# Engines lay out q and k, and the seven-product experts get other rooms, routes and an order

## Chip, core, metric

One core of a Trainium2 chip. The metric is device time in microseconds (us) of one execution of the whole program. TensorE (PE) does matmuls and transposes, VectorE is DVE, ScalarE is ACT, GpSimd is POOL, and SyncE (SP) issues every DMA of this program, in order.

## What is computed

The program is top-32 attention, a SiLU feed-forward layer, and eight ReLU experts weighted by a Sinkhorn-balanced gate, in fp32 precision.

```python
# q, k, v: (2, 8, 576, 64)
scores = q @ k.T / 8                       # per batch and head, 576 x 576
kth    = 32nd largest of each row
attn   = softmax(where(scores >= kth, scores, -1e9))
x      = (attn @ v) laid out as (1152, 512)
h = x @ w_in;  x = (h * sigmoid(h)) @ w_out          # 512 -> 2048 -> 512, float64 weights in DRAM
P = exp(x @ w_gate - max)                             # (1152, 8)
8 times: P /= row sums; P /= column sums; P *= 1152/8
out = sum over e of P[:, e] * (relu(x @ w1[e]) @ w2[e])   # 512 -> 1024 -> 512
```

## The kernel before, in words

**Attention** runs in 24 units (`units`, L589) of up to four score tiles; a unit is one pair of heads of one batch and one slice of query rows. For each score tile DVE finds the top 32 by four MAX8 and three MATCH_REPLACE (L304, L310), masks (L313), and ACT and PE do the rest. `load` brings q, k and v of a unit two units ahead. `turn_kv` and `turn_q` put q and k into the form that `score_tile` wants one unit ahead: two heads side by side, the fp32 value split into a high part (H, written by ACT) and the rest (L, written by DVE). PE transposes the natural tile, ACT and DVE empty PSUM into `kH, kL, qH, qL`, and then DMAs on the SP queue copy these from SBUF to SBUF into `kk`, `qq` and `qLz` (L236, L277 to L283). Only the first pair, named in `DIRECT`, is written by the engines directly.

**Feed-forward and experts of the early tokens.** There are nine token tiles of 128 rows. m0 (`row_ffn`, L640) is the layer for tile 0; it reads float64 weights, narrows them (`narrow`) and stores them in DRAM as `kept_in`, `kept_out`. Then `FILL[g]` follows after each group: six experts for tile 0 by `row_ffn`, then m1 (tiles 1, 2), expert 6 for tile 0 and expert 0 for tiles 1, 2, then m2 (tiles 3, 4) and expert 0 for tiles 3, 4. All of these use the same three PSUM `banks`, so on PE they follow each other in this order; this is called the chain of layers here. m3 (tiles 5 to 8) follows when attention is over. Then come the gate's Sinkhorn iterations (L720), and `AFTER`: expert 7 for tile 0 and expert 0 for tiles 5 to 8. Outputs of experts that can't be weighted yet go to DRAM (`ky`, L672, L778).

**The seven-product experts** (`ORDER`, L907): experts 7 to 1 on tiles 1 to 8, with the first layer done in blocks by seven products in place of eight. `pair_weights` loads raw weights (`raw_tile`, tag `raw`), forms sums on POOL (L810 to L813) and splits them into `wp` and `w2`. `pair_hidden` runs the seven products in the four PSUM banks `hb`; `first_half` and the loop over `yB` run the second layer. In the second of these experts (`i == 1`) all kept outputs are read back (`yk`, L913) through a pool of two tiles (`x1p`) and added on DVE (`weighted`, L892).

**What sets the order.** Tile writes each engine's instruction stream when the program is built, from priorities (`tc.cur_priority`, lower is earlier) and a modelled time; on the chip each stream runs in order. Work at `uid() * 100` comes first, then attention at 10 to 34 GAP, the layers, `AFTER` at 112 GAP, and `ORDER` at 300 GAP. Products of one expert have one priority, so the streams mix them.

Of the kernel before, what the change touches and what calls it, by code (L numbers as in the profile page):

```python
# [8 lines left out]
F32 = mybir.dt.float32  # L9
# [8 lines left out]
P = 128  # L18
# [6 lines left out]
    0: [(e, [0], "rows") for e in range(6)],  # L25
    1: [(6, [0], "rows"), (0, [1, 2], "split")],
# [7 lines left out]
DIRECT = [(0, 0)]  # L34

# [3 lines left out]
RW = 6  # L39
RWL = 5  # L40
# [4 lines left out]
KB = 2  # L45
# [17 lines left out]
def topk_attention_moe_sinkhorn_kernel(  # L63
# [121 lines left out]
    qq_half = [qtp.tile([P, 2, P], F32R, name=f"qq_half{i}", tag=f"qq_half{i}", bufs=1) for i in range(2)]  # L185
    qL_half = [qtp.tile([P, 2, P], F32R, name=f"qL_half{i}", tag=f"qL_half{i}", bufs=1) for i in range(2)]

    qLz = [qtp.tile([P, 2, 2 * P], F32R, name=f"qLz{i}", tag=f"qLz{i}", bufs=1) for i in range(2)]
    for t in qq_half + qL_half + qLz:
        nc.gpsimd.memset(t.bitcast(F32), 0.0)  # L190
    half_no = [0]
    full_no = [0]
# [16 lines left out]
    def turn_kv(b, p, kn, vn):  # L209

        kk = kvp.tile([P, 2, S], F32R, name=f"kk_{b}_{p}", tag="kk")
        direct = (b, p) in DIRECT
# [10 lines left out]
        if not direct:  # L223
            kH = nat.tile([P, S], F32R, name=f"kH_{b}_{p}", tag="kH", bufs=KB)
            kL = nat.tile([P, S], F32R, name=f"kL_{b}_{p}", tag="kL", bufs=KB)
# [7 lines left out]
        for src, hh in () if direct else ((kH, 0), (kL, 1)):  # L233
            for j in range(2):
                o = (j + hh) % 2 * 64
                nc.sync.dma_start(kk.bitcast(F32)[o : o + 64, j, :], src.bitcast(F32)[j * 64 : (j + 1) * 64, :])  # L236
        return kk, vn

    def load_q(b, p, t0, n, half):
        qn = nat.tile([P, 2, 2, D], F32, name=f"qn_{b}_{p}_{t0}", tag="qn")  # L240
        for j in range(2 if n else 0):
            nc.sync.dma_start(
                qn[:, 0:n, j, :],
                q[b, 2 * p + j, 0 : 4 * P, :].rearrange("(p c) d -> p c d", c=4)[:, t0 : t0 + n, :],
            )
        if half:
            nc.sync.dma_start(qn[0:64, 1, :, :], q[b, 2 * p : 2 * p + 2, 4 * P : S, :].rearrange("h p d -> p h d"))
        return qn

    def turn_q(b, p, t0, n, half, qn):  # L250

        w = n * P + (64 if half else 0)
        pq = ps_p.tile([P, 2 * P], F32, name=f"pq_{b}_{p}_{t0}", tag="pp")
        for c in range(n):
            nc.tensor.transpose(pq[:, c * P : (c + 1) * P], qn[:, c, :, :].rearrange("p h d -> p (h d)"), ident)
        if half:
            nc.tensor.transpose(pq[:, n * P : w], qn[0:64, 1, :, :].rearrange("p h d -> p (h d)"), ident[0:64, 0:64])
        low = qLz[full_no[0] % 2]
        full_no[0] += n > 0
        qq = qtp.tile([P, 2, 2 * P], F32R, name=f"qq_{b}_{p}_{t0}", tag="qq") if n else None  # L260
        if (b, p) in DIRECT and t0 == 0 and not half:
            for j in range(2):
                r = slice(j * 64, (j + 1) * 64)
                for o in (0, 64):
                    nc.scalar.activation(qq[o : o + 64, j, :w], pq[r, :w], AF.Copy)
                nc.vector.tensor_sub(low[r, j, :w], pq[r, :w], qq[r, j, :w].bitcast(F32))
            return qq, low, None
        qH = qtp.tile([P, 2 * P], F32R, name=f"qH_{b}_{p}_{t0}", tag="qH")
        qL = qtp.tile([P, 2 * P], F32R, name=f"qL_{b}_{p}_{t0}", tag="qL")
        evac_split(qH[:, :w], qL[:, :w], pq[:, :w])  # L270
        i = half_no[0] % 2
        half_no[0] += half
        for j in range(2):
            r = slice(j * 64, (j + 1) * 64)
            for o in (0, 64):
                if n:
                    nc.sync.dma_start(qq.bitcast(F32)[o : o + 64, j, : n * P], qH.bitcast(F32)[r, : n * P])  # L277
                if half:
                    nc.sync.dma_start(qq_half[i].bitcast(F32)[o : o + 64, j, r], qH.bitcast(F32)[r, n * P : w])
            if n:  # L280
                nc.sync.dma_start(low.bitcast(F32)[r, j, : n * P], qL.bitcast(F32)[r, : n * P])
            if half:
                nc.sync.dma_start(qL_half[i].bitcast(F32)[r, j, r], qL.bitcast(F32)[r, n * P : w])  # L283
        return qq, low, (qq_half[i], qL_half[i])
# [164 lines left out]
    def first_blocks():  # L449
# [5 lines left out]
        for i in (*range(13, nb), *reversed(range(13))):  # L455
            got[i] = cvp.tile([P, W], F32, name=f"wf_{i}", tag=f"wf{i}", bufs=1)
# [159 lines left out]
    for u, unit in enumerate(units):  # L616
# [19 lines left out]
        if g == 0:  # L636
# [49 lines left out]
    sk = left_pool("sk", bufs=2)  # L686
    m3s = ExitStack()
# [75 lines left out]

    for n, (e, ets) in enumerate(AFTER):
        tc.cur_priority = (112 + n) * GAP
        if ets == [0]:
            ys = [banks[2]]
            row_ffn(f"e{e}", x1F, ys[0], hidB(), expert_blocks(e), DFE // W, False, hp, hidB)
        else:
            ys = ys4  # L770
            ffn(f"e{e}_{ets[0]}", [x1_cols(ets)], ys, lambda f, m: fill_weights(e, f, "late"),
                DFE // P, False, hidB, hpB, late=True, depth=1)
        tc.cur_priority = uid() * 100
        for tt, y in zip(ets, ys):
            yo = x1p.tile([P, DM], F32, name=f"yo_{e}_{tt}", tag="x1")
            nc.scalar.activation(yo, y, AF.Copy)
            kept_y[e, tt] = drp.tile([P, DM], F32, name=f"ky_{e}_{tt}")
            nc.sync.dma_start(kept_y[e, tt], yo)  # L778
# [11 lines left out]
    wpp = left_pool("wpp", bufs=2)  # L790
    gbp = left_pool("gbp", bufs=NF)
    spp = left_pool("spp")
    rwl = left_pool("rwl", bufs=RWL)
# [46 lines left out]
    def pair_hidden(e, f, wd, hb, gB):  # L840

        nm = f"{e}_{f}"
        kept = tc.cur_priority

        def add(tag, a, ps, pool=upp, bufs=1):
            tc.cur_priority = uid() * 100
# [5 lines left out]
        block_product(hb[0], wd["a11"], b11)  # L852
        tc.cur_priority = uid() * 100
# [9 lines left out]
        block_product(hb[0], wd["a12"], b21, True)  # L863
        tc.cur_priority = uid() * 100
# [3 lines left out]
        h21 = add("h21", u2, hb[2])  # L868
# [11 lines left out]
    begun = set()  # L880

    def weighted(e, tt, y):

        p_ = pr[:, tt, e : e + 1]
        if tt not in begun:
            begun.add(tt)
# [19 lines left out]

    for i, e in enumerate(ORDER):  # L907
        tc.cur_priority = (300 + i) * GAP
        weights = [pair_weights(e, f) for f in range(NH)]
        if i == 1:  # L910
            for ek, tt in kept_y:
                yk = x1p.tile([P, DM], F32, name=f"yk_{ek}_{tt}", tag="x1")
                nc.sync.dma_start(yk, kept_y[ek, tt])  # L913
                weighted(ek, tt, yk)
# [4 lines left out]
        def first_half():  # L919
            f, gs, w2s = pend.pop(0)  # L920
            for n, (g, w) in enumerate(zip(gs, w2s)):
                product(yA, w, *g, f == 0 and n == 0, f == NH - 1 and n == 1)

        for f in range(NH):
            hb = group_of(i % 2, f"h_{e}_{f}")
# [46 lines left out]
```

## Time and profile before

| | us |
|---|---|
| median of 3 runs | 1327.61 (1327.47 to 1332.26) |
| profiled execution | 1326.74 |
| its span, first to last instruction | 1325.0 |
| PE busy | 1216.8 (92%) |
| DVE busy | 860.6 (65%) |
| ACT busy | 605.7 (46%) |
| POOL busy | 518.1 (39%) |
| mean busy share of the 16 DMA engines | about 39% |

The shares of the whole span hide the stages. In the slices of the page DVE is at 9 tenths up to about slice 16 while PE climbs, then PE alone is near full. PE's granted clock is at 5 tenths in the first slices and near full later. The rows below are read stage by stage.

### The profile page before, as it was taken

Reading aid. Unit: us, or ns where it says so; the run is one execution under the profiler, and the core shown is the slowest. Engines: PE = TensorE matmul, PEld = TensorE weight load, DVE = VectorE, ACT = ScalarE, POOL = GpSimd, SP = SyncE. Lnnn points to the kernel's source line nnn. Section 1 sums busy time; section 2 is a strip of 40 time slices with the busy share of each in tenths; the row PEclk is TensorE's granted clock in tenths of the full one; section 3 lists DMA queues with packets and bytes.
Section 4 is the critical chain, followed back from the end, with each engine's and each line's share of the span. In section 5 each row is a group of like instructions: output and inputs, shape, how many; then the busy total and the mean of one; then the engine's idle time right before and its main releaser. Section 6 shows DMA issues by size and latency. Waiting matters only on the chain.

```text
span 1325.0 us, 17423 instructions
## 1 busy us (share of the span) xinstructions
PE 1216.8 (92%) x5891; PEld 934.4 (71%) x5891; DVE 860.6 (65%) x1705; ACT 605.7 (46%) x1170; POOL 518.1 (39%) x464
## 2 busy tenths in 40 slices
PE   3669799979889988999998898999999999999998
PEld 2445455557758776889667686888888888888887
DVE  6999796979999999344474645445454454544533
ACT  4777454657768877543333323232232322323211
POOL 1443000016727766622353634335344353442510
PEclk7559799989999999999999999999999999999999
DMA  6999776665454533433422513112121121211101
GB/s 156 266 320 274 226 252 187 216 180 157 127 183 127 163 104 91 138 99 97 134 80 92 163 48 112 48 32 80 32 64 49 32 80 32 64 48 32 56 1 63
DMA packets 157288, 155.82 MB, mean 118 GB/s; under 512 B 34320, under 2 KB 109200, under 8 KB 157200
## 3 DMA queue, kind: packets, MB, share of 16 engines
q1 hardware_dynamic: 157200, 154.73, 39.0%
q8 instruction: 46, 0.75, 0.2%
q14 instruction: 42, 0.34, 0.1%
HBM read 128.73 MB, written 14.94 MB: 108 GB/s over the span
## 4 chain that ended last, share of the span: by engine, by line
PE 70%; DVE 12%; DMA 9%; ACT 4%; issue 2%; SPq 2%; POOL 1%; DVEq 0%; ACTq 0%; POOLq 0%
PE h L136 9%; PE h L138 8%; PE h L137 8%; PE bank L493 4%; PE yA L136 4%; PE yA L137 4%; DVE m L304 4%; PE yA L138 4%; DVE w L310 3%; PE yB L136 3%; PE yB L137 3%; PE bank L500 3%; PE yB L138 3%; PE bank L136 2%; PE bank L138 2%; PE bank L137 2%
## 5 line engine op out<-in xcount | busy, mean ns | idle before, releaser
L128 POOL TENSOR_TENSOR wp<-rw,wp 128x512 fp32r<-128x512 f32 (+1 forms) x56 | 83.4, 1508 | 183.6 <-ACT wp L127 183.6
L128 POOL TENSOR_TENSOR wa<-raw,wa 128x512 fp32r<-128x512 f32 x72 | 95.1, 1322 | 136.5 <-ACT wa L127 119.6
L304 DVE MAX8 m<-w 128x8 f32<-128x576 f32 x192 | 140.1, 746 | 0.2
L128 POOL TENSOR_TENSOR w<-rw,w 128x512 fp32r<-128x512 f32 x56 | 80.8, 1454 | 121.0 <-ACT w L127 120.5
L127 ACT ACTIVATE w<-rw 128x512 fp32r<-128x512 f32 x56 | 35.0, 629 | 133.6 <-PE yB L138 77.5
L310 DVE MATCH_REPLACE8 w<-m,w 128x576 f32<-128x576 f32 x128 | 94.6, 740 | 0.0
L447 POOL TENSOR_TENSOR wf<-wf,cv_n 128x512 int32<-128x512 int32 x32 | 43.0, 1344 | 83.2 <-ACT cv_n L444 35.1
L136 PE MATMUL h<-x1H,wp 128*128 128x512 f32 x168 | 68.1, 405 | 7.1 <-ACT p L855 6.8
L128 POOL TENSOR_TENSOR wb<-raw,wb 128x512 fp32r<-128x512 f32 x48 | 65.8, 1373 | 21.3 <-ACT wb L127 21.3
L835 DVE SCALAR_TENSOR_TENSOR gL_1b<-gB,gH_1b 128x512 fp32r<-128x512 f32 x28 | 38.4, 1371 | 50.7 <-issue 41.4
L137 PE MATMUL h<-x1L,wp 128*128 128x512 f32 x168 | 67.1, 400 | 0.0
L138 PE MATMUL h<-x1H,wp 128*128 128x512 f32 x168 | 67.1, 399 | 0.0
L313 DVE SCALAR_TENSOR_TENSOR s<-s,m,e 128x576 f32<-128x576 f32 x64 | 61.1, 955 | 0.2
L848 DVE TENSOR_TENSOR u<-p,h 128x512 f32<-128x512 f32 x28 | 19.2, 686 | 64.5 <-ACT p L855 64.5
L304 DVE MAX8 m<-s 128x8 f32<-128x576 f32 x64 | 48.0, 749 | 19.9 <-ACT s L296 19.9
L500 PE MATMUL bank<-wa,x1F 128*128 128x512 f32 x112 | 54.6, 623 | 6.3 <-DMA wa<-in_moe_w_dram 6.3
L127 ACT ACTIVATE wb<-raw 128x512 fp32r<-128x512 f32 x72 | 45.5, 632 | 30.2 <-PE y L138 15.9
L493 PE MATMUL bank<-wb,gT_e 128*128 128x512 f32 x128 | 58.2, 596 | 0.2 <-ACT gT_e L518 0.2
L330 PE MATMUL pav<-aT,vn 128*64 128x256 f32 (+3 forms) x480 | 53.0, 363 | 5.6 <-ACT aT L333 5.5
L308 ACT ACTIVATE e<-s,sm 128x576 f32<-128x576 f32 x64 | 49.7, 776 | 15.5 <-DVE s L313 12.2
L848 DVE TENSOR_TENSOR gB<-u,h 128x512 f32<-128x512 f32 x56 | 38.5, 687 | 25.3 <-PE h L138 23.4
L320 PE MATMUL pt<-ident,s 128*128 128x128 f32 x256 | 45.1, 305 | 9.2 <-ACT s L317 6.6
(355 smaller groups left out, 3757.1 us busy)
## 6 DMA issues: line engine op xcount, KB each, us to landing
rw<-in_moe_w_dram SPq DMA_DIRECT2D x112, 256.0 KB, 2.7
wa<-in_moe_w_dram SPq DMA_DIRECT2D x32, 512.0 KB, 4.7
wb<-in_moe_w_dram SPq DMA_DIRECT2D x32, 512.0 KB, 5.3
raw<-kept_in SPq DMA_DIRECT2D x48, 256.0 KB, 3.0
raw<-kept_out SPq DMA_DIRECT2D x48, 256.0 KB, 2.7
raw<-in_moe_w_dram SPq DMA_DIRECT2D x48, 256.0 KB, 2.8
wfr<-in_moe_w_in_dram SPq DMA_DIRECT2D x16, 512.0 KB, 5.0
wfr<-in_moe_w_out_dram SPq DMA_DIRECT2D x16, 512.0 KB, 6.1
```

The lines of the kernel that those rows point to most:

```text
L127: nc.scalar.activation(dH, src, AF.Copy)
L128: eng.tensor_sub(dL, src, dH.bitcast(F32))
L136: nc.tensor.matmul(ps, wH, xH, start=first, stop=False, skip_group_check=more)
L137: nc.tensor.matmul(ps, wH, xL, start=False, stop=False, skip_group_check=more)
L138: nc.tensor.matmul(ps, wL, xH, start=False, stop=last, skip_group_check=more)
L304: nc.vector.max(mr, src)
L310: nc.vector.match_replace(out=w, in_to_replace=mr, in_values=src, imm_value=-3e38)
L313: nc.vector.scalar_tensor_tensor(s, s, m8[:, TOPK - 1 : TOPK], e, op0=ALU.is_ge, op1=ALU.mult, accum_out=sm[:, 1:2])
L330: nc.tensor.matmul(ps[r, :n], vn[:, j, c, :], aT[j][:, c, :n], start=c == 0, stop=c == 4)
L493: nc.tensor.matmul(y, gT[:, c * P : (c + 1) * P], b[c], start=F == 0 and c == 0, stop=F == nF - 1 and c == NDC - 1)
L500: nc.tensor.matmul(ph, xF[:, c, :], a[c], start=c == 0, stop=c == NDC - 1)
L848: nc.vector.tensor_add(t, a, ps)
```

## The change

It has two parts that share no code.

In attention, `turn_kv` writes every pair of `k` straight from PSUM into `kk` as `DIRECT` did for one: each column range takes two ACT and two DVE instructions on 64 partitions in place of one each on 128, and the four DMA copies go. `turn_q` first lets POOL write each head's natural rows twice side by side (`qd`), so that a PE transpose brings the head out on both halves of the partitions; PE does a transpose per head and 128 rows in place of one for both heads, ACT and DVE empty twice the columns straight into `qq` and `qL`, and all DMA copies go. The natural q rows of a unit come by one DMA in place of two.

In the layers, expert 6 for tile 0 moves from behind m1 to in front of it. The seven-product experts load their raw weights into the pool `rwp` that the earlier layers use, and `wpp` is laid out ahead of m3's pools. `AFTER` leaves its outputs in `acc` by ACT, without DRAM, and POOL weights them there. The eleven other kept outputs are read back one at each of the first eleven steps `f`. Each product gets a priority of its own, 1000 above the one before. `p1` and `h21` share one tile. The order in which the narrowed weights are placed starts at 15 in place of 13.

```diff
 FILL = {
-    0: [(e, [0], "rows") for e in range(6)],
-    1: [(6, [0], "rows"), (0, [1, 2], "split")],
+    0: [(e, [0], "rows") for e in range(7)],
+    1: [(0, [1, 2], "split")],
...
-DIRECT = [(0, 0)]
...
-            if not direct:
-                evac_split(kH[:, cols], kL[:, cols], ps)
-                return
             for j in range(2):
                 r, o = (slice(i * 64, (i + 1) * 64) for i in (j, 1 - j))
                 nc.scalar.activation(kk[r, j, cols], ps[r], AF.Copy)
                 nc.vector.tensor_sub(kk[o, j, cols], ps[r], kk[r, j, cols].bitcast(F32))
...
-                nc.sync.dma_start(kk.bitcast(F32)[o : o + 64, j, :], src.bitcast(F32)[j * 64 : (j + 1) * 64, :])
...
+            nc.gpsimd.tensor_copy(dst[r], src[r][:, :, None, :].to_broadcast([r.stop, m, 2, D]))
+        qd = qd.rearrange("p (h c) e d -> p h c (e d)", c=2)
+        pq = ps_p.tile([P, 2, 2 * P], F32, name=f"pq_{b}_{p}_{t0}", tag="pp")
+        for j in range(2):
+            for c in range(n):
+                nc.tensor.transpose(pq[:, j, c * P : (c + 1) * P], qd[:, j, c, :], ident)
...
+            evac_split(qq[:, :, :w], qL[:, :, :w], pq[:, :, :w])
...
-                    nc.sync.dma_start(qq.bitcast(F32)[o : o + 64, j, : n * P], qH.bitcast(F32)[r, : n * P])
...
-                nc.sync.dma_start(low.bitcast(F32)[r, j, : n * P], qL.bitcast(F32)[r, : n * P])
...
+    wpp = left_pool("wpp", bufs=2)
     m3s = ExitStack()
     hpB = left_pool("hpB", m3s)
...
         for tt, y in zip(ets, ys):
-            yo = x1p.tile([P, DM], F32, name=f"yo_{e}_{tt}", tag="x1")
-            nc.scalar.activation(yo, y, AF.Copy)
-            kept_y[e, tt] = drp.tile([P, DM], F32, name=f"ky_{e}_{tt}")
-            nc.sync.dma_start(kept_y[e, tt], yo)
+            nc.scalar.activation(acc[:, tt, :], y, AF.Copy)
+            begun[tt] = e
...
-        raw = rwl.tile([P, W], F32, name=f"rw_{uid()}", tag="raw")
+        raw = rwp.tile([P, W], F32, name=f"rw_{uid()}", tag="raw")
...
+    def turn_on():
+        tc.cur_priority += 1000
+        return tc.cur_priority
+
     def block_product(ps, a, b, more=False):
+        turn_on()
...
-        if i == 1:
-            for ek, tt in kept_y:
+        if i == 0:
+            for tt, ek in begun.items():
+                nc.gpsimd.tensor_scalar(acc[:, tt, :], acc[:, tt, :], pr[:, tt, ek : ek + 1], 1.0,
+                                        op0=ALU.mult, op1=ALU.mult)
...
+        for f in range(NH):
+            if back:
+                ek, tt = back.pop(0)
                 yk = x1p.tile([P, DM], F32, name=f"yk_{ek}_{tt}", tag="x1")
                 nc.sync.dma_start(yk, kept_y[ek, tt])
                 weighted(ek, tt, yk)
```

## Rows read from the trace of the kernel before

**Rows 1.** Busy us by stage: length, PE, PEld, DVE, ACT, POOL, clock, DMA, GB/s.
```profile
25.00:143.00 118.00, 84.97 (x342) 53.18 (x342) 108.31 (x277) 83.26 (x161) 40.67 (x31) 0.68 0.86 263
...
250.00:310.00 60.00, 49.51 (x290) 32.08 (x289) 51.78 (x137) 34.80 (x81) 10.28 (x10) 0.94 0.58 165
310.00:525.00 215.00, 196.01 (x1247) 155.10 (x1246) 209.17 (x527) 165.84 (x353) 139.36 (x121) 0.99 0.46 136
...
721.00:740.00 19.00, 11.89 (x38) 8.56 (x37) 10.20 (x18) 10.39 (x18) 14.56 (x14) 0.82 0.73 224
...
831.00:1321.00 490.00, 489.94 (x2127) 398.83 (x2125) 233.77 (x282) 133.62 (x225) 188.74 (x169) 1.00 0.16 47
```

**Rows 2.** Chain that ended last, 120 to 146 us: start, us, what.
```profile
116.13 8.60 DMA wfr<-in_moe_w_out_dram
...
134.87 1.78 DMA qq_half<-qH
```

**Rows 3.** The same chain, 262 to 300 us.
```profile
283.26 0.47 SPq L277
...
288.69 3.62 DMA qn<-in_q_dram
...
295.75 4.05 DMA wa<-in_moe_w_dram
```

**Rows 4.** DMA issues of the program: tiles, count, size, median us to landing.
```profile
qq<-qH SPq DMA_DIRECT2D x48, 64.0 KB, 3.2
...
kk<-kH SPq DMA_DIRECT2D x14, 144.0 KB, 2.4
```

**Rows 5.** DVE groups by shape, 0 to 545 us: busy us, mean ns, idle before.
```profile
L132 DVE TENSOR_TENSOR qL<-pq,qH 128x256 fp32r<-128x256 f32 x12 | 5.0, 415 | 4.2 <-ACT qH L131 3.3 <-DMA qLz<-qL 0.9
L132 DVE TENSOR_TENSOR kL<-pk,kH 128x512 fp32r<-128x512 f32 x7 | 4.8, 680 | 0.1
...
L132 DVE TENSOR_TENSOR kL<-pk,kH 128x64 fp32r<-128x64 f32 x7 | 1.5, 208 | 0.0
...
L221 DVE TENSOR_TENSOR kk<-pk,kk 64x512 fp32r<-64x512 f32 x2 | 1.4, 688 | 7.0 <-ACT kk L220 7.0
```

**Rows 6.** Four PE transposes in a row, from the chain.
```profile
150.67 0.85 PE pt L320 x4
```

**Rows 7.** DVE groups by shape, 0 to 545 us: its only long idle time.
```profile
L128 DVE TENSOR_TENSOR wb<-raw,wb 128x512 fp32r<-128x512 f32 x1 | 1.7, 1730 | 9.8 <-POOL gL_e L128 9.8
```

**Rows 8.** Kept outputs of the chain of layers: min/median/max ns, first and last start.
```profile
L670 ACT ACTIVATE yo<-bank x11: 572/597/599, 181.8 to 559.2; 128x512 f32<-128x512 f32 x11
```

**Rows 9.** By shape: DVE's masking, 150 to 285 then 425 to 500 us; POOL, whole span.
```profile
L313 DVE SCALAR_TENSOR_TENSOR s<-s,m,e 128x576 f32<-128x576 f32 x14 | 11.3, 805 | 0.1
...
L313 DVE SCALAR_TENSOR_TENSOR s<-s,m,e 128x576 f32<-128x576 f32 x12 | 13.3, 1108 | 0.0
...
L128 POOL TENSOR_TENSOR wa<-raw,wa 128x512 fp32r<-128x512 f32 x72 | 95.1, 1322 | 136.5 <-ACT wa L127 119.6 <-DMA qn<-in_q_dram 13.4 <-PE bank L138 2.4
```

**Rows 10.** PE in order of time where the seven-product experts start; idle time in brackets.
```profile
724.47 0.60 PE L707 MATMUL pm_c<-cs,ones 128*128 128x8 f32 x2 [3.30 <-DVE cs L728]
725.32 0.79 PE L136 MATMUL h<-x1H,wp 128*128 128x512 f32 x1 [0.26 <-ACT yo L776]
...
738.26 0.51 PE L136 MATMUL h<-t2H,wp 128*128 128x512 f32 x1 [2.06 <-ACT wp L127]
```

**Rows 11.** SP, ACT and PE in order of time at the second such expert.
```profile
818.05 2.08 SPq L913 DMA_DIRECT2D yk<-ky  x2
...
821.94 0.42 SPq L801 DMA_DIRECT2D rw<-in_moe_w_dram  x1
...
827.17 0.80 PE L136 MATMUL h<-x1H,wp 128*128 128x512 f32 x1 [6.16 <-ACT p L855]
```

**Rows 12.** The chain at one same place of three successive experts.
```profile
790.07 0.91 PE yA L138 x4
...
880.63 0.91 PE yA L138 x4
...
963.59 0.91 PE yA L138 x4
```

More of the change, by code (lines that the diff above doesn't have):

```diff
@@ L39 @@
 RW = 6
-RWL = 5
 SB = 5
@@ L183, in topk_attention_moe_sinkhorn_kernel @@
     ps_p = att.enter_context(tc.tile_pool(name="ps_p", bufs=1, space=PSUM))
[L185 to L189, printed above, removed]
+    qq_half, qL_half = ([qtp.tile([P, 3 * P], F32R, name=f"{nm}_half{i}", tag=f"{nm}_half{i}", bufs=1)
+                         for i in range(2)] for nm in ("qq", "qL"))
+    for t in qq_half + qL_half:
         nc.gpsimd.memset(t.bitcast(F32), 0.0)
     half_no = [0]
-    full_no = [0]
     def load_kv(b, p):
@@ L245, in load_q @@
             )
         if half:
-            nc.sync.dma_start(qn[0:64, 1, :, :], q[b, 2 * p : 2 * p + 2, 4 * P : S, :].rearrange("h p d -> p h d"))
+            nc.sync.dma_start(qn[0:64, :, 1, :], qs[:, 4 * P : S, :].rearrange("h p d -> p h d"))
         return qn
     def turn_q(b, p, t0, n, half, qn):
[L252 to L255, printed above, removed]
@@ L256, in turn_q @@
-        if half:
[L257 to L267, printed above, removed]
@@ L284, in turn_q @@
-        return qq, low, (qq_half[i], qL_half[i])
+        w = n * P
+        qd = nat.tile([P, 4, 2, D], F32, name=f"qd_{b}_{p}_{t0}", tag="qd")
+        whole = qn.rearrange("p h c d -> p (h c) d")
+        parts = [(slice(0, P), whole, qd)] if n == 2 else []
+        if n == 1:
+            parts.append((slice(0, P), qn[:, :, 0, :], qd.rearrange("p (h c) e d -> p h c e d", c=2)[:, :, 0]))
+        if half:
+            parts.append((slice(0, 64), qn[:, :, 1, :], qd.rearrange("p (h c) e d -> p h c e d", c=2)[:, :, 1]))
@@ new lines, in turn_q @@
+        for r, src, dst in parts:
+            m = src.shape[1]
+            nc.gpsimd.tensor_copy(dst[r], src[r][:, :, None, :].to_broadcast([r.stop, m, 2, D]))
[4 more added lines that the diff above has]
+                nc.tensor.transpose(pq[:, j, c * P : (c + 1) * P], qd[:, j, c, :], ident)
+            if half:
+                nc.tensor.transpose(pq[:, j, w : w + 64], qd[0:64, j, 1, :], ident[0:64, 0:64])
@@ new lines, in turn_q @@
+        qq = qL = None
+        if n:
+            qq = qtp.tile([P, 2, 2 * P], F32R, name=f"qq_{b}_{p}_{t0}", tag="qq")
+            qL = qtp.tile([P, 2, 2 * P], F32R, name=f"qL_{b}_{p}_{t0}", tag="qL")
+            evac_split(qq[:, :, :w], qL[:, :, :w], pq[:, :, :w])
+        if not half:
+            return qq, qL, None
+        i = half_no[0] % 2
+        half_no[0] += 1
+        evac_split(*(t[i].rearrange("p (a b) -> p a b", b=192)[:, :, 0:64] for t in (qq_half, qL_half)),
+                   pq[:, :, w : w + 64])
@@ L454, in first_blocks @@
         got = {}
-        for i in (*range(13, nb), *reversed(range(13))):
+        for i in (*range(15, nb), *reversed(range(15))):
             got[i] = cvp.tile([P, W], F32, name=f"wf_{i}", tag=f"wf{i}", bufs=1)
@@ L646, in more @@
                 return mid.enter_context(tc.tile_pool(name=name, bufs=bufs, side="right", reuse_waits="tile"))
+            rwp = right.enter_context(tc.tile_pool(name="rwp", bufs=RW, side="right", reuse_waits="tile"))
             wap, wbp, hp = more("wap", WA), more("wbp", WB), more("hp", 2)
@@ L852, in pair_hidden @@
         block_product(hb[0], wd["a11"], b11)
+        kept = tc.cur_priority
         tc.cur_priority = uid() * 100
@@ L863, in pair_hidden @@
         block_product(hb[0], wd["a12"], b21, True)
+        kept = tc.cur_priority
         tc.cur_priority = uid() * 100
@@ L924, in topk_attention_moe_sinkhorn_kernel @@
         for f in range(NH):
+            if back:
+                ek, tt = back.pop(0)
+                yk = x1p.tile([P, DM], F32, name=f"yk_{ek}_{tt}", tag="x1")
+                nc.sync.dma_start(yk, kept_y[ek, tt])
+                weighted(ek, tt, yk)
             hb = group_of(i % 2, f"h_{e}_{f}")
```

50 lines of the change are left out of this document (15 added, 35 removed).

## The prediction

> **What bounds the kernel now.** I read the stage table first, because the shares of the whole span mix stages with different limits [rows 1]. From 831 us to the end PE is busy 489.94 of 490 us at full clock: this stage can only move as a whole, by starting earlier. From 310 to 525 us DVE works 209.17 of 215 us and PE 196.01: attention on DVE sets the pace, and PE fills its gaps with the chain of layers. From 25 to 143 us the DMA engines are busy for 0.86 of the time and DVE for 108.31 of 118 us. So the next question is which of DVE and PE ends late when attention is over. DVE has nothing left after about 533 us: its only long idle time before 545 us, 9.8 us, stands there [rows 7]. The chain of layers leaves its last output at 559.2 us [rows 8], and m3 needs both. PE, through the chain, is thus about 26 us behind DVE, and what counts ahead of m3 is when PE gets through its work.
>
> Then the chain of waits says where PE loses time. Ahead of 143 us it runs through the loads of m0's float64 weights (8.60 us for one) and, right at m0's last step, through a copy of q that holds ACT's stream (1.78 us) [rows 2]. From 262 to 300 us it runs through SP issuing copies (0.47 us each, seven such issues between 280.7 and 288.2 us), a q load (3.62 us) and the weights of expert 5 (4.05 us), which SP issued only at 295.75 us because the copies and small loads stood before them [rows 3]. In that stage PE is busy 49.51 of 60 us at 0.94 of full clock [rows 1]. Later, PE waits 3.30 us for the Sinkhorn chain and 2.06 us for the first seven-product weights [rows 10], and 6.16 us at 821 us [rows 11]. The last is put down to ACT's `p`, but ACT's stream stood behind a w2 load that SP issued at 821.94 us, after the read-back loads at 818.05 us that waited for a free `x1p` tile [rows 11]. That is the case for the change: several of PE's remaining waits are SP's order.
>
> **Part 1, up to 143 us (m0).** The copies in this stage are, by the code, 16 of k (144 KB) and about 36 of q, half of them of 64 KB and half of 32 KB [rows 4]: 2.3 + 1.7 = 4.0 MB. At the stage's 263 GB/s [rows 1] that is 15 us of DMA time. It is worth between nothing (m0 also waits for the first attention group, which DVE paces) and 15 us; the copy in the chain itself is 1.78 us [rows 2]. I take **-7**, half of it, because the chain goes through both DMAs and DVE.
>
> **Part 1, 250 to 310 us.** Here the copies go and SP issues weights when they are wanted. PE's idle time is 10.5 us, and the clock at 0.94 costs about 3.6 us of its work [rows 1]. Bounds 0 and -14. I take **-9**: the SP train is named by the chain. Expert 6, moved here, is the same PE work as before in another place: 0.
>
> **Part 1, what it adds.** PE: a transpose per head doubles them, 32 of 128 columns and 8 of 64 more. Four take 0.85 us [rows 6], so 32 x 0.21 + 8 x 0.1 = 7.5 us. Where PE has idle time this is free; after 143 us PE is near full. I take **+6.5** (bounds 0 and 7.5). DVE: for 7 of 8 pairs two subtractions of 64 partitions replace one of 128; 64x512 takes 688 ns against 680, and the 64-column piece about 208 [rows 5], so 7 x (2 x 0.90 - 0.89) = 6.4 us. For q, 512 columns replace 256 in 12 units, 680 against 415 ns [rows 5]: 3.2 us; the smaller units some 1.8. Together 11.4 us, hidden by the 26 us that DVE is ahead; without that cover it costs up to 11.4. Only the 8 units of the last two groups lie in the saturated stage (2.1 us), and PE waits there in order for scores: **+2**. ACT gains about as much work and isn't near its limit (165.84 of 215 us [rows 1]). POOL gets 24 copies `qd`. No such copy is in the trace; a subtraction of that size takes 1322 ns [rows 9], so 0 to 1.3 us each, I take 1.0 as a copy reads one tile in place of two, 24 us at most. They run a unit ahead of need: 0 here, and a rival below.
>
> One row bears on that: DVE's masking takes 805 ns while POOL is idle and 1108 ns while it is busy [rows 9]. The Trainium skill's page "SBUF — State Buffer", section "SBUF: two separate sides", says that VectorE and GpSimd share a pair of ports by an exclusive lock, which a VectorE instruction with two SBUF inputs can lose for a whole GpSimd instruction. By that rule the 24 copies lengthen masking, and the trace agrees in the 303 ns. From the rows alone: POOL is busy 139.36 of 215 us where masking loses about 0.3 us; 24 us more over some 430 us lifts the loss by 0.03 us for each of 72 tiles, 2 us on DVE, under the cover.
>
> **Part 2, start of the seven-product experts.** In 721 to 740 us PE is busy 11.89 of 19 us at a clock of 0.82 [rows 1]: 7.1 us idle and 3.4 us of clock. With weights in their own room and no DRAM trip for `AFTER`'s outputs, the first product waits for ACT to empty banks, four copies of 0.6 us [rows 8], 2.2 us with the hand-over. That leaves 4.9 us of idle time saved, and I count 2.1 of the 3.4 us of clock: **-7** (bounds 0 and -10). If Sinkhorn's last matmul stays ahead of the products in PE's stream, the 3.30 us stay, and that is what is late next. The DRAM trips cost SP ten issues less.
>
> **Part 2, read-backs one by one.** The same place of successive experts is 90.56 us apart and then 82.96 us [rows 12]; the difference holds the 6.16 us and the half clock behind it. **-7.6** (bounds 0 and -7.6): one `yk` a step has its two tiles free in time, and the w2 loads don't queue behind it. POOL's five scalings in place, up to 1.3 us each, are behind the weights of the first pairs; if put ahead of them, 6.6 us.
>
> **Part 2, order.** Work per expert is the same 360 matmuls, 0.230 us each. With strict order, products that reuse a bank after two others have 2.8 us for an ACT copy (0.6) or a DVE addition (0.69) [rows 5, 8]; a DVE busy with something else eats that slack now and then. Nothing to gain where PE is full: **+1** (0 to +8).
>
> **Sum.** -7 - 9 + 6.5 + 2 - 7 - 7.6 + 1 = -21.1 us on an execution of 1326.74 us (span 1325.0): 1305.6, and the median of the runs lies 0.9 us above this execution: **1306 us**.
>
> **The rivals.** (a) Part 1 relieves nothing that PE waits for: m0 is held by DVE and the expert weights by DMA bandwidth. Then -16 goes and the added work stays: 1322. For it: PE is full from 143 to 250 us anyway; against: the copies are in the chain by name. (b) Part 2 changes no wait: the raw tiles of `AFTER` and of expert 7 share six buffers, so that the weights are late as before. Then -14.6 goes: 1320. For it: POOL idles ahead of these weights today for ACT alone; against: raw loads and `wpp` no longer wait for m3's pools. (c) **Slower**: POOL is now on q's way to PE. In 310 to 525 us POOL is busy 139.36 of 215 us with subtractions of 1.3 us [rows 1, 9], its stream is in order, and a late `qd` holds the transposes, and behind these on PE the scores and the chain of layers. Two or three subtractions late in each of the last ten units is 3 us x 10: 1336. It decides from 2.2 us per unit on. Against: a unit of lookahead is about 25 us. (d) The shared ports at their worst: every copy stops DVE for its whole length, 24 x 1.3 = 31 us, with the 11.4 us 17 more than the cover: 1323. Against: the masking lost 0.3 us, not 1.3. (e) That it doesn't do what it says can't be here in full, for the copies are gone from the code; (b) is its half.
>
> **How the numbers follow.** The forecast has 0.60, (a) 0.13, (b) 0.12, (c) 0.10, (d) 0.05. About 0.5% (6.6 us) is what a measurement of this kernel can tell from no change: faster is below 1321, slower above 1334. The forecast lies below nearly whole, (b) for two thirds and (a) for a good third: faster 0.75. (c) gives slower 0.11 with the tails; 0.14 is left for the same. The range takes the forecast with its bounds down to 1288 (the first two terms near their ends) and goes up over (a), (b) and (d) to 1325; it leaves out (c) and some of the lower tail.
>
> **What would show it.** Right: m0's last step before 138 us; expert 5's output before 300 us and PE over 55 of 60 us there; the last kept output of the chain before 553 us; no PE idle time over 2.5 us between `AFTER` and the experts; seven equal steps of 83 us. Wrong: PE waiting for POOL at `pq` (c); DVE still busy with attention when the chain is through (the cover gone); steps longer than 83 us (order).

## The result, and the profile after

| us | before | after |
|---|---|---|
| median | 1328.01 (1327.47 to 1332.26) | 1298.78 (1297.10 to 1300.48) |
| profiled execution, and its span | 1326.74, 1325.0 | 1297.10, 1295.2 |

The ratio is 0.9773 (95% interval 0.9749 to 0.9797). The forecast was 1306 us, with 1288 to 1325 as its range: the time came out 7 us below it. Term by term it was less close. Places that both programs have are ACT's copies of a layer's outputs out of PSUM: m0 has one such copy, m3 and the last layer of `AFTER` have four each, of which the start of the first is taken. Between such places the 29.8 us of the two spans are:

| from, to | before | after | difference | forecast |
|---|---|---|---|---|
| start to m0's output | 143.0 | 143.0 | 0.0 | -7 |
| m0's to m3's first output | 501.4 | 487.1 | -14.3 | -9 + 6.5 + 2 |
| m3 to the last layer of `AFTER` | 76.0 | 76.0 | 0.0 | 0 |
| that layer to the first `yB` product | 72.2 | 64.9 | -7.3 | -7 |
| first to second expert's `yB` | 90.57 | 82.75 | -7.8 | -7.6 |
| the five steps after it | 414.9 | 413.8 | -1.2 | +1 |
| last expert's first `yB` to the end | 26.9 | 27.7 | +0.8 | 0 |

One execution of `at_once_sixteen` below, 1391.19 us at a granted clock of 0.843 against 0.976 in its three others, is left out there.

The stages of the kernel after, with the columns of [rows 1] (length, PE, PEld, DVE, ACT, POOL, clock, DMA share, GB/s):

```profile
25.00:143.00 118.00, 78.69 (x349) 50.51 (x350) 116.62 (x286) 83.98 (x158) 45.76 (x40) 0.83 0.73 250
100.00:125.00 25.00, 22.46 (x81) 12.70 (x78) 24.75 (x61) 13.31 (x25) 2.30 (x4) 0.87 0.07 26
143.00:250.00 107.00, 104.22 (x463) 58.35 (x461) 100.23 (x250) 63.57 (x128) 3.73 (x8) 1.00 0.64 200
250.00:310.00 60.00, 59.82 (x311) 37.63 (x311) 51.19 (x127) 38.44 (x87) 18.45 (x20) 1.00 0.60 190
310.00:525.00 215.00, 198.07 (x1323) 164.36 (x1322) 212.45 (x533) 172.06 (x370) 152.16 (x136) 0.98 0.38 109
...
707.00:726.00 19.00, 17.04 (x75) 13.79 (x75) 14.11 (x23) 9.27 (x17) 15.53 (x14) 1.00 0.50 148
771.00:1290.00 519.00, 518.48 (x2257) 423.66 (x2256) 227.91 (x296) 145.92 (x241) 195.09 (x179) 1.00 0.16 48
```

In 250 to 310 us PE is full at full clock, where it had 10.5 us of idle time [rows 1]. Up to 143 us it is the other way: the DMA engines are done early (0.07 of their time from 100 to 125 us, where it was 0.92), yet m0 ends no sooner, and DVE is now busy 116.62 of 118 us, against 108.31 [rows 1]. The chain of waits points at DVE too. Where it went through `wfr` loads and the copy `qq_half` [rows 2], it is now DVE's work from 60 us up to `gr_m`, m0's first gate, but for a gap of 0.59 us; from there to 126 us it is mostly PE's products of m0:

```profile
102.76 1.32 DVE s L294 x2
104.08 1.46 DVE w L291 x3
105.60 1.33 DVE m L285 x2
106.99 0.60 DVE gr_m L489
```

m0 needs the first attention group. ACT's copy of that group's last output, in the kernel before and then after:

```profile
92.32 0.28 ACT L369 ACTIVATE x<-pav 128x128 f32<-128x128 f32 x1
```
```profile
101.02 0.28 ACT L350 ACTIVATE x<-pav 128x128 f32<-128x128 f32 x1
```

It comes 8.7 us later, and m0's steps behind it take 42.0 us in place of 50.6, since POOL is through with the last weight at 103.5 us in place of 130.8. So the relief of the DMAs did arrive, and the later group took it back.

The kept outputs of the chain of layers, as in [rows 8], with the first and last start in us:

```profile
L652 ACT ACTIVATE yo<-bank x11: 576/597/598, 174.8 to 534.2; 128x512 f32<-128x512 f32 x11
```

The last one stands at 534.2 us in place of 559.2; DVE's last masking of attention ends at 531.1 us (532.7 before). Of the 26 us by which DVE was ahead, 3 are left. At the seven-product experts PE waits 2.07 us for Sinkhorn, in place of 3.30 [rows 10], and then runs through; the same place of three experts comes 82.75 us apart from the first, where [rows 12] have 90.56 and then 82.96:

```profile
708.96 0.39 PE L690 MATMUL pm_c<-cs,ones 128*128 128x8 f32 x2 [2.07 <-DVE cs L711]
709.21 0.48 PE L132 MATMUL h<-x1H,wp 128*128 128x512 f32 x1
```
```profile
807.35 0.70 PE yA L134 x3
...
890.10 0.70 PE yA L134 x3
...
972.86 0.70 PE yA L134 x3
```

At the very end a new wait has come: the last output tile is free only when a store has landed.

```profile
1288.26 2.25 DMA out_dram<-o
1290.62 0.51 DVE o L880
```

### The profile page after: what moved, and what is told of

Read it like the earlier page. It is cut to its first block, busy times and chain, and to the rows that moved or that the text cites. A ratio compares the mean times of both kernels' runs of the same rounds, so it can differ in the third digit from the quotient of the medians.

```text
span 1295.2 us, 17189 instructions
## 1 busy us (share of the span) xinstructions
PE 1200.7 (93%) x5931; PEld 928.9 (72%) x5931; DVE 854.8 (66%) x1722; ACT 615.4 (48%) x1180; POOL 526.0 (41%) x495
## 4 chain that ended last, share of the span: by engine, by line
PE 68%; DVE 21%; issue 5%; ACT 3%; POOL 2%; DMA 1%; SPq 0%; DVEq 0%; POOLq 0%; ACTq 0%
PE h L134 8%; PE h L132 8%; PE h L133 8%; DVE m L285 7%; DVE w L291 6%; PE yB L133 4%; PE yB L132 4%; PE yB L134 4%; PE yA L134 4%; PE yA L133 4%; PE yA L132 4%; PE bank L474 3%; PE bank L481 3%; PE bank L132 3%; PE bank L133 3%
## 5 line engine op out<-in xcount | busy, mean ns | idle before, releaser
L124 POOL TENSOR_TENSOR wp<-rw,wp 128x512 fp32r<-128x512 f32 (+1 forms) x56 | 86.9, 1571 | 203.7 <-ACT wp L123 203.6
L124 POOL TENSOR_TENSOR wa<-raw,wa 128x512 fp32r<-128x512 f32 x72 | 95.4, 1325 | 119.7 <-ACT wa L123 117.6
L124 POOL TENSOR_TENSOR w<-rw,w 128x512 fp32r<-128x512 f32 x56 | 73.4, 1314 | 81.8 <-ACT w L123 81.8
L246 POOL COPY qd<-qn 128x512 f32<-128x512 f32 (+2 forms) x28 | 14.8, 535 | 144.3 <-issue 105.6
L298 ACT ACTIVATE s<-s,sm 128x576 f32<-128x576 f32 x64 | 50.0, 782 | 24.1 <-DVE sm L297 22.9
L301 PE MATMUL pt<-ident,s 128*128 128x128 f32 x256 | 43.0, 295 | 16.1 <-ACT s L298 15.3
L124 DVE TENSOR_TENSOR wp<-sp,wp 128x1024 fp32r<-128x1024 f32 x28 | 45.8, 1636 | 14.0 <-ACT wp L123 13.9
```

Of the source, the lines that this page charges most:

```text
L124: eng.tensor_sub(dL, src, dH.bitcast(F32))
L298: nc.scalar.activation(s, s, AF.Copy, scale=sm[:, 3:4])
```

## The experiments

The theory was the forecast's: PE waited for what SP's order held up, through copies, read-backs and rooms. The rivals: DVE sets the early part (then the copies' DMA time is worth little there); and, since every engine's stream is planned anew at each build, a wait may go because the streams mix otherwise, not because its named cause is gone. The table gives the same stretches for each kernel, from its profiled execution; the first step is the one from the first to the second expert's `yB`.

| kernel | m0's output | m0 to m3 | `AFTER` to `yB` | first step | span |
|---|---|---|---|---|---|
| before | 143.0 | 501.4 | 72.2 | 90.57 | 1325.0 |
| after | 143.0 | 487.1 | 64.9 | 82.75 | 1295.2 |
| att_only | 144.1 | 488.6 | 74.8 | 90.13 | 1315.3 |
| exp_only | 143.1 | 500.2 | 65.7 | 82.75 | 1308.9 |
| six_rows | 144.5 | 491.5 | 65.7 | 82.75 | 1302.0 |
| q_low_pool | 145.5 | 485.9 | 65.7 | 82.75 | 1298.5 |
| back_at_once | 143.9 | 487.5 | 65.7 | 82.75 | 1297.4 |
| no_order | 144.4 | 487.2 | 65.7 | 82.75 | 1297.5 |
| old_rooms | 145.1 | 486.4 | 68.1 | 83.66 | 1302.8 |
| at_once_sixteen | 144.3 | 487.5 | 67.5 | 82.75 | 1299.3 |
| copies_pool_queue | 163.5 | 497.3 | 74.5 | 88.79 | 1345.9 |
| no_shift_before | 136.8 | 487.2 | 72.8 | 83.39 | 1298.0 |
| no_shift_after | 138.0 | 485.6 | 66.2 | 82.75 | 1291.2 |
| four_outs | 144.0 | 487.8 | 64.9 | 82.75 | 1295.2 |

A difference of up to 1.5 us in m0's end says little: in `no_order` and `four_outs` every engine has the same records in the same order as in the kernel after (by operation, tile name and shape), and m0's output comes 1.4 and 1.0 us later. From `AFTER` to `yB` 0.8 us says little for the same reason.

### One part alone

The attention part without the experts' (`att_only`), and the reverse (`exp_only`, with expert 6 moved as in the change). The core of the first, against the kernel after:

```diff
-    0: [(e, [0], "rows") for e in range(7)],
-    1: [(0, [1, 2], "split")],
+    0: [(e, [0], "rows") for e in range(6)],
+    1: [(6, [0], "rows"), (0, [1, 2], "split")],
...
-        raw = rwp.tile([P, W], F32, name=f"rw_{uid()}", tag="raw")
+        raw = rwl.tile([P, W], F32, name=f"rw_{uid()}", tag="raw")
```

> The kernel before with the attention part of the change alone: q and k laid out by engines, no copies, one load of q; layers and experts as before. Theory (the 14.3 us that m3 ends earlier come from SP's relief in attention, the rest from the experts): 1328 - 14 = 1314, the expert stage as long as before, m3's end near 630 us. Rival 1 (they come from moving expert 6 ahead of m1, which isn't here): 1325 to 1332, since the transposes and DVE's added work stay. Rival 2 (the two parts need each other): over 1318.

> The kernel after with the attention of the kernel before: copies by SP, everything else changed. Theory: 1328 - 15 = 1313: m3 ends near 644 us as before, the stage from there to the end is 15 us shorter. Rival 1 (expert 6's new place brings the early gain): 1299 to 1304. Rival 2 (the chip gains the sum only together): over 1318.

Measured: 1316.97 us, 0.9933 (0.991 to 0.9957), and 1312.93 us, 0.9902 (0.9873 to 0.9932) of the kernel before. Each part acts where it should: the first takes 12.8 us from m0 to m3 and 0.4 us from the first step, the second takes 6.5 us from the experts' start and 7.8 us from the step, and 1.2 us from m0 to m3. Spans fall by 9.7 and 16.1 us, 4.0 less than by both together. Most of that is in one place: with attention alone the experts' start is 2.6 us longer than before, which the whole change doesn't show.

### Expert 6 in its old place

```diff
-    0: [(e, [0], "rows") for e in range(7)],
-    1: [(0, [1, 2], "split")],
+    0: [(e, [0], "rows") for e in range(6)],
+    1: [(6, [0], "rows"), (0, [1, 2], "split")],
```

> The kernel after with expert 6 for tile 0 behind m1 again. Theory (its place changes nothing, as its work on PE is the same): within 1.5 us of after. Rival (its place fills the stretch ahead of m1, whose weights and chains would wait otherwise, and leaves m3's start to attention alone): slower by 2 to 6 us.

Measured: 1302.43 us, 0.9819 (0.9784 to 0.9855), 3.7 us above the kernel after, as the rival had it. m0 to m3 takes 4.4 us longer, and the chain's last output is 16.7 us later (550.9 us). The prediction had this move at 0, since the work is the same. From m0 to m3 PE's idle time is 1.0 us longer than in the kernel after and its time at half clock (granted clock 0.5, 1.2 of 2.4 GHz) 3.4 us longer, which is 2.7 of the 4.4 us; why isn't shown. With the reverse experiment (`exp_only`, 1.2 us) the move is worth 1 to 4 us.

### Where attention's DVE work ends

q's low part made on POOL out of an fp32 copy by ACT, so that q's subtractions leave DVE:

```diff
-            evac_split(qq[:, :, :w], qL[:, :, :w], pq[:, :, :w])
+            q32 = nat.tile([P, 2, 2 * P], F32, name=f"q32_{b}_{p}_{t0}", tag="q32")
+            nc.scalar.activation(q32[:, :, :w], pq[:, :, :w], AF.Copy)
+            split(qq[:, :, :w], qL[:, :, :w], q32[:, :, :w])
```

> The kernel after with the low part of q formed by POOL from an SBUF copy that ACT makes; DVE loses 24 subtractions, about 11 us up to 530 us, ACT and POOL gain as many instructions. Theory (DVE, through attention, is what m3 now waits for): attention ends 5 to 10 us earlier and m3 2 to 6 us earlier, 1293 to 1297. Rival (PE's chain of layers is still the bound): m3 ends within 1.5 us of after, 1297 to 1301. Second rival (shared ports, POOL in q's way): slower, over 1303.

Measured: 1301.03 us, 0.9811 (0.9777 to 0.9845). Attention's DVE work ends at 526.6 us, 4.5 us earlier, and m3 no earlier (631.4 against 630.1 us); the chain's last output comes at 540.0 us. So although only 3 us of the cover are left, DVE's end isn't seen to hold m3, and no cost of the change's added DVE work shows there. What DVE's work costs earlier is the next question.

### Less DVE work ahead of m0

The 32 left shifts of the narrowing are taken out, of the kernel before and of the one after:

```diff
         t = x.bitcast(I32)
-        nc.vector.tensor_scalar(t, t, 3, None, op0=ALU.logical_shift_left)
         nc.gpsimd.tensor_add(t, t, n)
```

> The kernel after without the 32 shifts by which DVE narrows the float64 weights; this step of the computation is left out, 16 us of DVE work ahead of 143 us. Theory (DVE took the place of the DMAs as the bound of the stretch up to m0's end, which is why m0 ends at 143 us in both kernels): the first attention group ends 8 to 14 us earlier, m0 6 to 12 us earlier, and the whole 5 to 10 us. Rival (m0's own chain of ACT, POOL and PE steps holds it): m0 ends within 3 us of 143 us.

> The kernel before without the same 32 shifts, the same step of the computation left out. Theory (here the weight loads hold m0): m0 ends within 4 us of 143 us although the first attention group ends earlier, the whole 1 to 6 us faster. Rival (DVE was the bound of this stretch before the change too): m0 ends 6 us earlier or more.

Measured: 1293.89 us, 0.9758 (0.9717 to 0.9799), for the one from after: the first attention group ends 7.1 us sooner, m0 at 138.0 us, 5.0 us sooner, and most of that is kept to the end. Each is a little less than expected. The shifts were 16 us of DVE's time, so a third of it comes through: DVE's work holds m0 in the kernel after, though not alone.

For the one from before: 1301.34 us, 0.9816 (0.9767 to 0.9864), some 26 us less, far more than expected. m0 ends 6.2 us sooner, as the rival had it: DVE's work held m0 before the change too, and the weight loads were not its only limit. Then m0 to m3 takes 14.2 us less, in a stretch with no shift in it, and the first step 7.2 us less, in a part of the program that wasn't touched. In 250 to 310 us PE has 5.8 of the 10.3 us that the change brought (49.51 before [rows 1], 59.82 after), with all the copies still there. The stage ahead of it in the kernel before, and then both stages in this one:

```profile
143.00:250.00 107.00, 101.71 (x428) 57.77 (x427) 89.47 (x228) 57.14 (x112) 1.48 (x2) 0.95 0.75 240
```
```profile
143.00:250.00 107.00, 102.20 (x461) 58.75 (x460) 100.85 (x260) 59.95 (x123) 0.40 (x2) 0.97 0.73 236
250.00:310.00 60.00, 55.28 (x330) 36.97 (x329) 53.30 (x140) 39.93 (x93) 18.67 (x17) 0.97 0.64 189
```

SP's queue shows how. The lines are start, us, what SP issued. In the kernel before SP was issuing almost without a break from 274 us, and the weights `wa` that PE wanted followed at 295.75 us [rows 3]. Here most such copies stand ahead of 272 us, between expert weights:

```profile
258.60 0.47 SPq L479 DMA_DIRECT2D wa<-in_moe_w_dram  x1
...
260.72 1.77 SPq L277 DMA_DIRECT2D qq<-qH  x3
262.59 0.54 SPq L281 DMA_DIRECT2D qLz<-qL  x1
...
266.83 0.82 SPq L479 DMA_DIRECT2D wa<-in_moe_w_dram  x1
...
273.14 0.47 SPq L479 DMA_DIRECT2D wa<-in_moe_w_dram  x1
```

PE's waits for q at 281 us and for `wa` at 298 us are gone; one of 3.33 us for `wa` stands at 260 us. So the prediction's reading was right in that SP's order made these waits, and wrong in that the copies must go for that. Which of the 14.2 us are the new order and which the 13 us by which attention is ahead after m0 (its DVE work ends 376.4 us behind m0, against 389.7) this run can't tell: taking out one line of DVE work planned all streams anew.

### The copies in another queue

The kernel before with its copies of q and k issued by POOL, one of five such edits:

```diff
-                nc.sync.dma_start(kk.bitcast(F32)[o : o + 64, j, :], src.bitcast(F32)[j * 64 : (j + 1) * 64, :])
+                nc.gpsimd.dma_start(kk.bitcast(F32)[o : o + 64, j, :], src.bitcast(F32)[j * 64 : (j + 1) * 64, :])
```

> The kernel before with the copies of q and k issued from POOL's queue in place of SP's; the copies and all else stay. Theory (SP's order, not the copies' transfer time, held the experts' weights at 250 to 310 us): expert 5's output moves from 310 to under 295 us and m3 ends 5 to 11 us earlier, 1317 to 1322. Rival (transfer and latency of the copies hold the scores): expert 5's output stays over 303 us and the time is 1325 or more, since POOL's own work is held by issuing.

Measured: 1345.52 us, 1.0147 (1.0104 to 1.019): slower by 1.5%. Expert 5's output comes at 298.1 us, between theory and rival. The row experts (those of tile 0) do come closer behind m0 (the sixth ends 134.6 us behind it, against 166.8), but by m3 only 4.1 us of that are left, and m0 itself is 20.5 us late. POOL takes 0.52 us for each issue, in the stage in which it also narrows weights. DVE loses more. Groups by shape (busy us, mean ns), in the kernel before from 25 to 143 us:

```profile
L304 DVE MAX8 m<-w 128x8 f32<-128x576 f32 x45 | 33.0, 747 | 0.0
...
L446 DVE TENSOR_SCALAR wf<-wf 128x512 int32<-128x512 int32 x30 | 15.2, 506 | 6.0 <-ACT wf L442 6.0
L313 DVE SCALAR_TENSOR_TENSOR s<-s,m,e 128x576 f32<-128x576 f32 x16 | 13.7, 854 | 0.0
```

and in this kernel from 25 to 163 us, with POOL's issues below:

```profile
L304 DVE MAX8 m<-w 128x8 f32<-128x576 f32 x49 | 35.9, 746 | 0.0
...
L313 DVE SCALAR_TENSOR_TENSOR s<-s,m,e 128x576 f32<-128x576 f32 x16 | 23.4, 1464 | 0.0
L446 DVE TENSOR_SCALAR wf<-wf 128x512 int32<-128x512 int32 x30 | 20.5, 683 | 2.3 <-ACT wf L442 2.2
```
```profile
L277 POOL DMA_DIRECT2D qq<-qH x32 | 16.5, 522 | 8.1 <-PE ps L293 3.9 <-ACT qH L131 3.8 <-ACT x L369 0.4
```

MAX8 takes what it took; masking, which reads two tiles in SBUF, goes from 854 to 1464 ns, and the shift from 506 to 683. That is 9.8 + 5.3 = 15 us more on an engine that is busy 130.57 of these 138 us. The issues themselves don't lengthen masking. Two maskings, and what POOL does beside each:

```profile
85.03 3.19 DVE L313 SCALAR_TENSOR_TENSOR s<-s,m,e 128x576 f32<-128x576 f32 x1
...
121.39 0.81 DVE L313 SCALAR_TENSOR_TENSOR s<-s,m,e 128x576 f32<-128x576 f32 x1
```
```profile
85.10 2.50 POOL L447 TENSOR_TENSOR wf<-wf,cv_n 128x512 int32<-128x512 int32 x2
...
121.12 1.56 POOL L277 DMA_DIRECT2D qq<-qH  x3
```

The three maskings beside issues alone take 0.79 to 0.81 us; the six that take over 1 us (1.80 to 3.19) all stand beside POOL's additions of the narrowing, 1.3 us each, of which the kernel before has as many. What the issues change seems to be when these additions run; no run separates that. The lock of the Trainium skill's page "SBUF — State Buffer", section "SBUF: two separate sides", quoted in the prediction, fits that masking suffers beside the additions and MAX8 doesn't; that the shift with its one input suffers too isn't in what is quoted there.

### Read-backs: spread, rooms, order, route

Four kernels undo one or two things each of the kernel after: the read-backs all in the second expert (`back_at_once`), the raw weights and `wpp` in their old pools (`old_rooms`), the line that raises each product's priority left out (`no_order`), and the read-backs all at once with `AFTER`'s outputs among them by DRAM, sixteen as before (`at_once_sixteen`):

```diff
-            nc.scalar.activation(acc[:, tt, :], y, AF.Copy)
-            begun[tt] = e
+            yo = x1p.tile([P, DM], F32, name=f"yo_{e}_{tt}", tag="x1")
+            nc.scalar.activation(yo, y, AF.Copy)
+            kept_y[e, tt] = drp.tile([P, DM], F32, name=f"ky_{e}_{tt}")
+            nc.sync.dma_start(kept_y[e, tt], yo)
...
+        if i == 1:
+            for ek, tt in back:
+                yk = x1p.tile([P, DM], F32, name=f"yk_{ek}_{tt}", tag="x1")
+                nc.sync.dma_start(yk, kept_y[ek, tt])
+                weighted(ek, tt, yk)
```
```diff
-        raw = rwp.tile([P, W], F32, name=f"rw_{uid()}", tag="raw")
+        raw = rwl.tile([P, W], F32, name=f"rw_{uid()}", tag="raw")
```
```diff
     def turn_on():
-        tc.cur_priority += 1000
         return tc.cur_priority
```

> The kernel after with its eleven kept outputs read back together at the second seven-product expert, as before. Theory (w2 loads stand behind read-backs on SP): slower by 4 to 8 us, with a PE wait of some us in the second expert's first steps; eleven instead of sixteen read-backs make it a little less than the 7.6 us of before. Rival (the wait came from late weights in general, which the new rooms cure): within 1 us of after.

> The kernel after with the raw tiles, their pool and the product weights' pool back where they were before the change. Theory (early weights are worth the clock drop and the idle time at the start of the experts): slower by 4 to 7 us, all between 707 and 771 us. Rival (AFTER's outputs staying in SBUF free the banks early, and that alone is the gain there): within 1.5 us of after.

> The kernel after without the growing priority of the products (the line that adds 1000 is gone), so that the products of an expert mix again. In the kernel with the read-backs put together the second expert still took 82.75 us, so something else cured its 7.6 us. Theory (order cures it: products in order need w2 later, and spread the loads): the step to the second expert is over 86 us, the later steps 82.99 us, together 4 to 9 us slower than after. Rival (eleven read-backs in place of sixteen, or the new ring of raw tiles, cure it): all steps under 83.1 us and the whole 1 to 2 us slower than after.

> The kernel after with AFTER's five outputs going through DRAM again and all sixteen kept outputs read back together at the second seven-product expert, as before the change; new rooms and order stay. Neither eleven read-backs together nor mixed products brought the 7.6 us back. Theory (the five outputs of AFTER cause it: they take the two x1p tiles late, so that the other read-backs and the w2 loads behind them come late): the step to the second expert is over 85 us and AFTER's hand-over 1 to 2 us longer, together 4 to 9 us slower than after. Rival (the rooms and the ring of raw tiles cure it): all steps under 83.1 us, at most 2 us slower.

Measured: 1299.24 (0.9802, 0.9777 to 0.9828), 1304.82 (0.9839, 0.9814 to 0.9865), 1299.20 (0.9794, 0.9753 to 0.9834) and 1300.30 us (0.9805, 0.9757 to 0.9853). The step stays at 82.75 us in three of them and is 83.66 us with the old rooms; none brings 90.57 back. So the step needs neither the spread read-backs, since sixteen asked for together don't hurt, nor the new rooms, since with the old ones and spread read-backs 0.9 us are lost and not 7.8. With all of it undone (`att_only`) the step is 90.13.

The order of the products stays a rival, for none of the four undoes it. `no_order` has the same records in the same order as the kernel after on every engine, so it is in effect a repeat of that kernel and no test: against its expectation, its products don't mix. Over the 360 matmuls of a step PE goes from one product to another 54 to 56 times in the kernel after and in every kernel with its experts' part, `no_order` among them, and 132 to 136 times in the kernels with a wait there (before, `att_only`, `copies_pool_queue`: 88.79 to 90.57 us). Against the order as the only cure stands `no_shift_before`, which mixes products too (105 times in that step) and takes 83.39 us.

SP's queue shows the wait in `att_only`: the w2 load that ACT wants stands behind read-backs that come in as tiles get free (SP's lines first, then ACT's):

```profile
807.90 1.98 SPq L895 DMA_DIRECT2D yk<-ky  x2
809.97 0.38 SPq L783 DMA_DIRECT2D rw<-in_moe_w_dram  x1
811.60 0.32 SPq L895 DMA_DIRECT2D yk<-ky  x1
811.97 0.42 SPq L783 DMA_DIRECT2D rw<-in_moe_w_dram  x1
```
```profile
814.98 0.63 ACT L124 ACTIVATE w<-rw 128x512 fp32r<-128x512 f32 x1 [8.02 <-DMA rw<-in_moe_w_dram]
815.52 0.58 ACT L837 ACTIVATE p<-h 128x512 f32<-128x512 f32 x1
```

That is the pattern of [rows 11], and the reading was right. In `at_once_sixteen` SP has six weight loads out ahead of the last read-backs:

```profile
783.13 1.70 SPq L908 DMA_DIRECT2D yk<-ky  x2
784.92 12.05 SPq L784 DMA_DIRECT2D rw<-in_moe_w_dram  x6
797.14 0.99 SPq L908 DMA_DIRECT2D yk<-ky  x2
```

What is worth something at the experts' start is in the other columns. Kernels with neither undone lie at 64.9 to 66.2 us. The old rooms lose 1.9 to 3.2 us there (68.1), and 2.1 us more from m3 to `AFTER` (78.1 in place of 76.0), not all between 707 and 771 us as expected. The DRAM route of `AFTER`'s outputs loses 1.3 to 2.6 (67.5): PE then waits 3.85 us for Sinkhorn in place of 2.07.

### The tail

The last output tiles of tokens 5 to 7 in rooms that are free by then, in place of the two `x1p` tiles:

```diff
-            o = x1p.tile([P, DM], F32, name=f"o_{tt}", tag="x1")
+            pool, tag = {5: (upp, "p1"), 6: (upp, "u2"), 7: (upp, "u3")}.get(tt, (x1p, "x1"))
+            o = pool.tile([P, DM], F32, name=f"o_{tt}", tag=tag)
```

> The kernel after with free tiles for three of the last four outputs, so that none waits for an earlier output's DMA: after's time from PE's end to the end of the span is 5.8 us, with 1.72 us of DVE waiting for a DMA. Theory: 1.5 to 2 us faster than after, in the tail alone, too little for the interval. Rival (the four output DMAs queue anyway): the tail stays within 0.5 us of 5.8 us.

Measured: 1297.92 us, 0.9788 (0.9747 to 0.9829). From PE's last product to the end it takes 4.0 us, as before the change, in place of 5.8: the 1.8 us are gone in the trace. On the whole time they can't be told from the 1.7 us by which m3 happened to come later, on streams that are the same up to there.

## Why the prediction was right, and where it wasn't

**Up to m0's end (-7; 0.0 measured).** This step failed. The DMA time of the copies did go, as the 0.07 of 100 to 125 us shows, but the stage had two near limits, and the prediction took half of one of them without asking what the other allowed. DVE had 9.7 us free of 118 [rows 1]. The weights came earlier and the first attention group ended later (101.0 us against 92.3): up to its end DVE did 31 of the 32 shifts in place of 21, 4.8 us more, and 3.5 us more of subtractions for q and k, work that the change adds or brings forward. `no_shift_after` and `no_shift_before` show that DVE's work counts in both kernels: 5.0 and 6.2 us of m0 for 16 us of it. The prediction's 26 us of cover, read at 533 to 559 us, didn't hold at 143 us. The count of copies was off as well: the trace has 55 of q up to 143 us, not about 36.

**250 to 310 us (-9) with the added PE (+6.5) and DVE work (+2): -14.3 measured from m0 to m3.** Right in kind, mis-sized. PE's idle time in that stretch falls from 34.8 to 21.6 us and its time at half clock from 20.5 to 6.8, which is 6.9 us of work at full clock: -13.2 - 6.9 + 6 of transposes is -14.1. The relief of 20 us lies beyond the bound of 14, because the step looked only at the stage that the chain named, with 10.5 us of idle time, and (a) calls PE full from 143 to 250 us, where it was busy 101.71 of 107 us at a clock of 0.95. PE lost time there too: from m0's to the sixth row expert's output it has 15.8 us of idle time and 17.1 at half clock, and in the kernel after, up to the seventh's, 3.0 and 0. DVE's +2 isn't seen (`q_low_pool`).

**Expert 6's place (0; -1 to -4).** Counted as the same work elsewhere; `six_rows` (4.4 us) and `exp_only` (1.2 us) show that the place has a price.

**Start of the experts (-7; -7.3).** Right, and for its reasons: from `AFTER` to `yB` PE's idle time falls from 7.1 to 2.5 us, and the 3.4 us that half clock cost it are gone, where 4.9 and 2.1 were counted. `old_rooms` and `at_once_sixteen` show the rooms and the DRAM route at 1.9 to 3.2 and 1.3 to 2.6 us; what makes the rest of the 7.3 isn't separated. Sinkhorn's wait stayed, as the prediction allowed, at 2.07 us.

**Read-backs (-7.6; -7.8).** The size is right and the wait was the one named. But the cure that it names, "one `yk` a step has its two tiles free in time", isn't needed: `back_at_once` and `at_once_sixteen` have no such spread and no wait, and `no_shift_before` loses the wait with this part untouched. That it is the place of one load in SP's order fits them all. Which edit moved it, the products' order among them, stays open.

**Order (+1; -1.2) and the end (0; +0.8).** The later steps are 0.24 us shorter each, not longer. That goes with the order of the products, 82.75 us in every kernel that keeps them apart and 82.95 to 83.05 in every one that mixes them, but no run changes the order alone. The 1.8 us of the tail were not foreseen: the kernel now ends through two tiles with stores in flight (`four_outs`). The last expert's second layer, 1.0 us shorter, gives back the rest.

**The rivals.** (a), that part 1 relieves nothing and DVE holds m0, held up to m0 and not behind it. (b) fell with the start and the step. (c), POOL in q's way, fell: the copies `qd`, 28 of them and not 24, take 514 ns in the median, half of the 1.0 us taken, 14.8 us in all, and PE is seen to wait for them once, 2.1 us. (d) fell with them: masking takes 971 ns in the mean, against 955 before.

```profile
L246 POOL COPY qd<-qn x28: 389/514/1142, 6.8 to 378.9; 128x512 f32<-128x512 f32 x12, 128x256 f32<-128x256 f32 x8, 64x256 f32<-64x256 f32 x8
```
```profile
L294 DVE SCALAR_TENSOR_TENSOR s<-s,m,e 128x576 f32<-128x576 f32 x64 | 62.2, 971 | 0.1
```

Of the signs, expert 5's output (280.2 us), PE in its stage (59.82 of 60), the chain's last output (534.2), the 2.07 us and the equal steps came as told; m0's end before 138 us did not. That the sum was near is in part luck: -7 too much and some 14 too little.

**Open** stays how much of the 14.3 us from m0 to m3 needs the copies gone. Removing them alone gave 12.8 (`att_only`); a new order with less DVE work ahead of m0 gave 14.2 with the copies in place. No kernel here held the order fixed.

## What to carry to other kernels

Where two engines are near full in a stage, what the relief of one brings is bounded by the slack of the other in that same stage, and slack that an engine shows at the end of a phase need not be there earlier. A wait behind a queue that issues in order has more than one cure (fewer issues, more room, another order), so name the load that is late and what stands ahead of it; which edit moved it takes an experiment with the rest held. Where streams are planned at each build, an edit is compared with its undoing by stretches between common places, for it moves waits in parts that it doesn't touch. Compare the streams too: an edit that leaves them as they were, as `no_order` does, tests nothing.

## What the runs showed of the hardware

DMA issues on POOL's queue took 0.52 us each, where SP's of the same copies `qq` took 0.59 in the median. DVE's masking beside such issues alone took 0.79 to 0.81 us, and up to 3.19 us beside POOL's additions; MAX8 kept its 746 ns in that kernel. POOL's fp32 copy of 128x512 took 685 ns in the mean, where its subtraction of that size takes 1322 [rows 9]. The kernel before varied more than the one after: 21 executions of it beside these runs lay between 1318.72 and 1330.91 us at mean granted clocks of 0.951 to 0.981, the four of after between 1297.10 and 1300.48 at 0.974 to 0.980. With PE's early waits went most of its time at half clock between m0 and m3.
